# One line of due steps for ScalarE, VectorE and GpSimd, with their shared port in the planner, and epsilon added on ScalarE

## The chip, the cores and the metric

One core of one Trainium2 chip runs the whole program. The metric is device time in microseconds (us), the median of several executions of one compiled kernel. The engines are named as the profile names them: PE is TensorE, DVE is VectorE, ACT is ScalarE, POOL is GpSimd, SP issues the transfers.

## The reference

Local attention with a few global columns, followed by two feed-forward layers, all in float32:

```
attention: B=2, H=8, S=768, D=64; a query sees itself and the 95 keys before it, and the first 8 keys
  scores = q k^T / 8 - slope_h * distance, masked; a = exp(scores - max); a = a / (sum(a) + 1e-9); x = a v
layer 1:   1536 tokens, 512 -> 1536 -> 512:   x = ((x w_a) * (x w_b)) w_out
layer 2:   1536 tokens, 512 -> 2048 -> 512:   h = x w_in
           g = h where h >= 1, 0 where h <= -1, else (h + 1)^2 / 4;   out = g w_out
```

The weights arrive as float64. The matmuls of the two layers keep float32 accuracy by splitting each operand into a high and a low part and adding three products.

## The kernel before

**Work.** The 1536 tokens are three tiles of 512 (`t` = 0, 1, 2). Attention is cut into 24 units, each two heads by 256 queries; eight units make the input of one tile. A unit goes through PE and the other engines in turn: scores on PE (L681); mask, scale and row minimum on DVE out of PSUM (`least`, L698); four `exp` on ACT (L710); epsilon added to the four row sums (`add`, L718) and their reciprocal (`inverse`, L721) on DVE; four multiplications of rows by it (`norm`, L737) on POOL or DVE; transposes on PE (L745) and their copy out of PSUM on ACT or DVE; values on PE (L762); high part (ACT or DVE) and low part (DVE, L644) of the layer's input. Three units may be in flight.

A block of weights (`prep`, 68 of them, 128x512 each) is turned from float64 into a high and a low float32 by a chain of seven steps: L378 on ACT, L379 to L382 on DVE (L379 may be on POOL), a rounding copy `w_hlh` (L391 on DVE, L389 on ACT) and a subtraction `w_hll` (L384, on POOL or DVE). Only twelve such blocks have a place until the first product of the third tile. Products of a layer are 12 matmuls of 512 columns; the results are taken out of PSUM by `after_ab` and `evacuate` (L505, L519, L522, L527, L563) and split into `midh` and `midl` (L391/L389 and L410).

**Order.** Everything is emitted as one static program. A planner, `Clock`, decides the order while the program is built. It keeps a model time in ns; PE's part of the program advances it by `MM` for each matmul. Every step of the other three engines is handed to `Clock.on` with a slack (which gives its due time), its cost on each engine that could do it, and a function that tells when it may go. In the kernel before, `on` fixes the engine at once: it takes the one with the least sum of busy time, queued earlier-due work, cost and a handicap (`BIAS`, or `BIAS_W` for steps of slack 1900 and more; on DVE 900 and 1000 ns). `begin` then serves three separate queues by due time whenever the model says that an engine is free. Steps of DVE and POOL never exclude each other in this model. Each engine runs its instructions strictly in the order emitted, and waits by semaphores. PE's order is decided in `tile_kernel`: a step of the attention goes before the next matmul of a layer when it is due or when that matmul's operands are not there yet in the model.

The numbers that the change touches:

```
MM = 216
BIAS = dict(scalar=100, vector=900, gpsimd=0)
BIAS_W = dict(scalar=2700, vector=1000, gpsimd=200)
SLACK = dict(
    qk=400, reduce=0, exp=0, share=-800, norm=1000, turn=0, x=0, evac=1000, mid=3500, y=100, weights=500, soon=1900,
)
```

Of the kernel before, what the change touches and what calls it, by code (L numbers as in the profile page):

```python
# [2 lines left out]

# [11 lines left out]
AF = mybir.ActivationFunctionType  # L15
# [31 lines left out]
TINY, HUGE = 3.0517578125e-05, 122880.0  # L47


MM = 216  # L50
COPY = dict(scalar=520, vector=335)
COPY_PS = dict(scalar=478, vector=602)
SUB = dict(vector=602, gpsimd=1225)
CLAMP = dict(vector=335, gpsimd=1883)

BIAS = dict(scalar=100, vector=900, gpsimd=0)
BIAS_W = dict(scalar=2700, vector=1000, gpsimd=200)

HOP = dict(tensor=200, scalar=160, vector=170, gpsimd=120)
DMA = dict(issue=475, begin=1125, rate=360, end=900)  # L60
# [47 lines left out]
class Clock:  # L108

    ENGINES = ("scalar", "vector", "gpsimd")

    def __init__(self, nc):
        self.nc = nc
        self.now, self.seq, self.events = 0, 0, []
        self.busy = dict.fromkeys(self.ENGINES, 0)
        self.queue = {e: [] for e in self.ENGINES}
        self.dma_issue = self.dma_busy = -1 << 20  # L120
        self.poll = lambda: None

# [1 line left out]
        self.seq += 1  # L124
        heapq.heappush(self.events, (self.now + ns, self.seq, fn))

    def on(self, slack, emit, then=None, need=None, **costs):


        def end(e):  # L130
            ahead = sum(op[2] for op in self.queue[e] if op[0] <= self.now + slack)
            return max(self.busy[e], self.now) + ahead + costs[e] + (BIAS if slack < SLACK["soon"] else BIAS_W)[e]

        e = min(costs, key=end)
        self.seq += 1
        self.queue[e].append((self.now + slack, self.seq, costs[e], emit, then, need))

    def begin(self):

        more = True  # L140
        while more:
            more = False
            for e in self.ENGINES:
                if self.busy[e] > self.now:
                    continue
                for op in sorted(self.queue[e], key=lambda op: op[:2]):
                    _, _, ns, emit, then, need = op
                    if need and not need():
                        continue
                    self.queue[e].remove(op)  # L150
                    emit(getattr(self.nc, e))
                    self.busy[e] = self.now + ns
                    self.after(ns, lambda: None)
                    if then:
                        self.after(ns + HOP[e], then)
                    more = True
                    break

    def dma(self, n, then):
        issued = max(self.dma_issue, self.now)  # L160
# [127 lines left out]
class Ffn:  # L288
# [194 lines left out]
    def after_ab(self, kind, t, f, n, ps, room):  # L483
        clock = self.clock
        give = lambda: self.give(room)
        if kind == "a":
            a = []

            def emit(e):
                self.take("s1")  # L490
                a.append(self.p_s.tile([P, T], F32, tag="s1", name=f"a{n}"))
                self.copy(e, a[0], ps)

            def there():
                give()
                self.a[t, f] = a[0]

            clock.on(SLACK["evac"], emit, there, self.has("s1"), **COPY_PS)
        elif kind == "b":
            ab = []  # L500

            def emit(e):
                self.take("s2")
                ab.append(self.p_s.tile([P, T], F32, tag="s2", name=f"ab{n}"))
                e.tensor_tensor(ab[0], ps, self.a.pop((t, f)), ALU.mult)  # L505

            def there():
                give()
                self.give("s1")
                self.split_mid(("y", t, f), ab[0])  # L510

            clock.on(SLACK["evac"], emit, there, lambda: self.room["s2"] > 0 and (t, f) in self.a, vector=602)
        else:
            c, g = [], []

            def clip(e):
                self.take("s1")
                c.append(self.p_s.tile([P, T], F32, tag="s1", name=f"c{n}"))
                e.tensor_scalar(c[0], ps, -1.0, 1.0, ALU.max, ALU.min)  # L519

            def square(e):
                e.activation(c[0], c[0], AF.Square, bias=self.half, scale=0.5)  # L522

            def larger(e):
                self.take("s2")
                g.append(self.p_s.tile([P, T], F32, tag="s2", name=f"g{n}"))
                e.tensor_tensor(g[0], ps, c[0], ALU.max)  # L527

            def there():
                give()  # L530
                self.give("s1")
                self.split_mid(("o", t, f), g[0])

            s = SLACK["evac"]
            third = lambda: clock.on(s, larger, there, self.has("s2"), vector=602)
            second = lambda: clock.on(s, square, third, scalar=613)
            clock.on(s, clip, second, self.has("s1"), vector=598)

    def evacuate(self, kind, t, first, last, e, ps, cols):
        nc, clock = self.nc, self.clock  # L540
        if first:

            def copy(en):
                self.part[kind, t, e] = part = self.p_part.tile([P, T], F32, tag="part", name=f"{kind}part{t}_{e}")
                self.copy(en, part, ps)

            clock.on(SLACK["evac"], copy, lambda: self.give("acc"), **COPY_PS)
            return
        part = self.part[kind, t, e]

        def there():
            self.give("acc")
            if not last:
                return
            if kind == "o":
                row = t * T + e * P
                nc.sync.dma_start(self.out[row : row + P, cols], part[:, cols])
                return
            if t not in self.y:
                self.y[t] = self.new_x(f"y{t}")  # L560
            self.split(SLACK["y"], lambda: self.y[t][e], part, lambda at: self.ready.add(("h", t, e)))

        add = lambda en: en.tensor_tensor(part[:, cols], ps[:, cols], part[:, cols], ALU.add)  # L563
        clock.on(SLACK["evac"], add, there, vector=602)

    def prepare(self):

# [43 lines left out]
class Attention:  # L611
# [20 lines left out]
    def to_x(self, ps, t, p, col, w):  # L632

        ready, clock = self.ffn.ready, self.clock

        def then():
            self.give(ps)
            self.done[t, p] = self.done.get((t, p), 0) + w
            if self.done[t, p] == T:
                ready.update((kind, t, p) for kind in "ab")  # L640

        places = [a[:, col : col + w] for a in self.ffn.x[t][p]]
        hi = lambda e: self.ffn.copy(e, places[0], ps[:, :w])
        lo = lambda e: e.tensor_tensor(places[1], ps[:, :w], as_f32(places[0]), ALU.subtract)  # L644
        low = lambda: clock.on(SLACK["x"], lo, then, vector=335)
        clock.on(SLACK["x"], hi, low, scalar=264, vector=335)


class Window(Attention):
# [38 lines left out]
    def reduce(self, st, j, r, ps):  # L688
        clock = self.clock
        at, w = self.places(st)[r]  # L690
        i = st["i0"] + r
        m0 = (0, P, P + self.W)[min(i, 2)]
        pt, stat = st["p", j][:, at : at + w], st["stat"]
        n = NQ * j + r
        most, total = stat[:, 0, n : n + 1], stat[:, 1, n : n + 1]

        def least(e):
            e.tensor_tensor_reduce(  # L698
                pt, ps[:, at : at + w], self.masks.m[:, m0 : m0 + w], scale=-(0.5 ** (2 * st["p"] + j + 1)),
                scalar=3e38, op0=ALU.add, op1=ALU.min, accum_out=most,  # L700
            )

        def reduced():
            st["read", j] = st.get(("read", j), 0) + 1
            if st["read", j] == NQ:
                self.give(ps)
            clock.on(SLACK["exp"], exp, share, scalar=2 * w)

        def exp(e):
            e.activation(pt, pt, AF.Exp, bias=most, scale=-1.0, accum_out=total)  # L710

        def share():
            st["exp"] = st.get("exp", 0) + 1
            if st["exp"] == 2 * NQ:
                clock.on(SLACK["share"], add, lambda: clock.on(SLACK["share"], inverse, norms, vector=81), vector=70)

        def add(e):
            e.tensor_scalar_add(stat[:, 2], stat[:, 1], EPS)  # L718

        def inverse(e):  # L720
            e.reciprocal(stat[:, 2], stat[:, 2])  # L721

        def norms():
            for jj in range(2):
                for rr in range(NQ):
                    clock.on(SLACK["norm"], *self.norm(st, jj, rr), gpsimd=457, vector=202)

        clock.on(SLACK["reduce"], least, reduced, lambda: not i or not self.masks.left, vector=w * 4 // 3)

    def norm(self, st, j, r):  # L730
        at, w = self.places(st)[r]
# [7 lines left out]
    def turn(self, st, j):  # L739
# [9 lines left out]
            st["turned", j] = True  # L749

        copy = lambda e: self.ffn.copy(e, pt[:, :n], ps[:, :n])
        self.write(n * 110 // P, lambda: clock.on(SLACK["turn"], copy, out, scalar=52 + n * 5 // 6, vector=n * 7 // 6))

    def values(self, st):

# [366 lines left out]
```

## Time and profile before

| | |
|---|---|
| median of 3 runs | 666.62 us (664.29 to 666.94) |
| profiled execution | 665.21 us, of it 663.3 us from the first to the last instruction |
| busy: PE / DVE / ACT / POOL | 642.2 / 463.5 / 199.4 / 236.5 us |
| share of PE in the chain that ended last | 81%; DVE 15% |
| granted PE clock, mean | 0.991 |

Busy times are those of the profiled execution. PE's busy time holds the latency of each matmul and is no measure of how full PE is; the steps of the chain that ended last are. A DVE or POOL instruction that stands still while it holds its engine counts as busy.

### The profile page before, as it was taken

How to read it: one execution, taken by the hardware profiler on the slowest of the kernel's cores; microseconds unless marked ns; L12 is line 12 of the kernel's file. 1: busy time of each engine (PE TensorE's matmuls, PEld its weight loads, DVE VectorE, ACT ScalarE, POOL GpSimd, SP SyncE). 2: the span in 40 equal slices, each digit the busy share in tenths (PEclk: the TensorE clock that was granted, in tenths of full speed). 3: DMA queues.
4: the chain of work that ended last, by engine and by line, in shares of the span. 5: the costliest groups of instructions: out<-in, count | busy, mean ns of one | idle time of the engine just before them, and what ended most of it. 6: DMA issues, size and time to landing. Idle time of an engine off the chain costs nothing.

```text
span 663.3 us, 9060 instructions
## 1 busy us (share of the span) xinstructions
PE 642.2 (97%) x3190; PEld 514.1 (78%) x3190; DVE 463.5 (70%) x966; ACT 199.4 (30%) x458; POOL 236.5 (36%) x239
## 2 busy tenths in 40 slices
PE   6988899999999999999999999999999999999997
PEld 3665677778878888888888878888888888888886
DVE  7999966427792755982737997894699778944442
ACT  5766755542221201211212134333221212111110
POOL 4655744023252331331333445444241423222220
PEclk7899999999999999999999999999999999999999
DMA  7765652101341221430211330322121211000112
GB/s 218 221 199 171 178 174 74 48 1 64 96 126 33 63 64 33 127 96 0 68 59 41 120 95 1 127 65 64 33 96 63 65 40 56 0 1 17 48 49 84
DMA packets 23766, 52.71 MB, mean 79 GB/s; under 512 B 3104, under 2 KB 11552, under 8 KB 23712
## 3 DMA queue, kind: packets, MB, share of 16 engines
q1 hardware_dynamic: 23568, 52.05, 25.6%
q8 instruction: 27, 0.44, 0.3%
q14 instruction: 27, 0.22, 0.1%
q10 hardware_dynamic: 144, 0.00, 0.0%
HBM read 48.89 MB, written 3.15 MB: 78 GB/s over the span
## 4 chain that ended last, share of the span: by engine, by line
PE 81%; DVE 15%; issue 1%; ACT 0%; POOL 0%; DVEq 0%; POOLq 0%
PE ps L446 42%; PE o L474 20%; PE y L474 13%; PE at L762 2%; DVE p L698 2%; DVE bits L381 2%; PE at L681 2%; PE at L745 2%; DVE bits L382 1%; DVE bits L380 1%; DVE w_hlh L391 1%; DVE p L737 1%; DVE bits L379 1%; DVE midh L391 1%; DVE ab L505 1%
## 5 line engine op out<-in xcount | busy, mean ns | idle before, releaser
L384 POOL TENSOR_TENSOR w_hll<-bits,w_hlh 128x512 fp32r<-128x512 f32 x46 | 65.8, 1431 | 92.0 <-DVE w_hlh L391 83.5
L446 PE MATMUL ps<-xhx,w_hlh 128*128 128x512 f32 x224 | 88.5, 395 | 0.0
L446 PE MATMUL ps<-xlx,w_hlh 128*128 128x512 f32 x224 | 88.4, 394 | 0.0
L446 PE MATMUL ps<-xhx,w_hll 128*128 128x512 f32 x224 | 88.0, 393 | 0.0
L522 ACT ACTIVATE c<-c,half 128x512 f32<-128x512 f32 x48 | 34.8, 724 | 153.5 <-DVE c L519 153.5
L505 DVE TENSOR_TENSOR ab<-ps,a 128x512 f32<-128x512 f32 x34 | 23.4, 688 | 65.1 <-PE ps L446 65.1
L446 PE MATMUL ps<-xhy,w_hll 128*128 128x512 f32 x168 | 65.4, 389 | 0.0
L446 PE MATMUL ps<-xly,w_hlh 128*128 128x512 f32 x168 | 65.4, 389 | 0.0
L446 PE MATMUL ps<-xhy,w_hlh 128*128 128x512 f32 x168 | 65.4, 389 | 0.0
L378 ACT ACTIVATE bits<-raw 128x512 f32<-128x512 f32 x68 | 44.9, 669 | 64.0 <-POOL w_hll L384 43.3
L410 POOL TENSOR_TENSOR midl<-g,midh 128x512 fp32r<-128x512 f32 x25 | 33.6, 1344 | 84.2 <-DVE midh L391 84.2
L519 DVE TENSOR_SCALAR c<-ps 128x512 f32<-128x512 f32 x48 | 32.9, 686 | 42.1 <-PE ps L446 42.1
L382 DVE SCALAR_TENSOR_TENSOR bits<-raw,bits 128x512 uint32<-128x512 uint32 x68 | 52.6, 777 | 0.9
L527 DVE TENSOR_TENSOR g<-ps,c 128x512 f32<-128x512 f32 x48 | 33.1, 689 | 27.1 <-ACT c L522 25.6
L410 POOL TENSOR_TENSOR mid_morel<-g,mid_moreh 128x512 fp32r<-128x512 f32 x21 | 28.8, 1369 | 62.4 <-DVE mid_moreh L391 57.4
L381 DVE SCALAR_TENSOR_TENSOR bits<-raw,bits 128x512 uint32<-128x512 uint32 x68 | 49.6, 735 | 0.6
L446 PEld LDWEIGHTS ps<-xhx,w_hlh 128*128 128x128 f32 x224 | 42.1, 188 | 9.7 <-issue 1.7
L446 PEld LDWEIGHTS ps<-xlx,w_hlh 128*128 128x128 f32 x224 | 42.1, 188 | 8.9 <-issue 1.0
L446 PEld LDWEIGHTS ps<-xhx,w_hll 128*128 128x128 f32 x224 | 42.1, 188 | 8.6 <-issue 0.3
L389 ACT COPY a<-ps 128x512 f32<-128x512 f32 x34 | 19.9, 585 | 88.3 <-PE ps L446 84.5
L410 POOL TENSOR_TENSOR midl<-ab,midh 128x512 fp32r<-128x512 f32 x15 | 19.6, 1306 | 59.6 <-DVE midh L391 58.8
L380 DVE TENSOR_SCALAR bits<-bits 128x512 uint32<-128x512 uint32 x68 | 40.0, 593 | 0.9
(296 smaller groups left out, 1477.6 us busy)
## 6 DMA issues: line engine op xcount, KB each, us to landing
raw<-in_wu SPq DMA_DIRECT2D x68, 512.0 KB, 3.6
v<-in_vd SPq DMA_DIRECT2D x16, 256.0 KB, 3.8
k<-in_k SPq DMA_DIRECT2D x16, 200.0 KB, 3.8
q<-in_qd SPq DMA_DIRECT2D x48, 64.0 KB, 3.7
out<-opart SPq DMA_DIRECT2D x11, 256.0 KB, 2.0
k<-in_k SPq DMA_DIRECT2D x8, 128.0 KB, 3.5
v<-in_vd SPq DMA_DIRECT2D x8, 128.0 KB, 3.5
v<-in_vd SPq DMA_DIRECT2D x8, 64.0 KB, 3.4
```

What stands on the lines that cost most here:

```text
L378: (lambda e: e.activation(as_f32(b), as_f32(high), AF.Abs), dict(scalar=520)),
L380: (lambda e: e.tensor_scalar(b, b, 3, 0x3FFFFFF8, shl, both), dict(vector=335)),
L381: (lambda e: e.scalar_tensor_tensor(b, low, 29, b, shr, or_), dict(vector=602)),
L382: (lambda e: e.scalar_tensor_tensor(b, high, 0xC0000000, b, both, or_), dict(vector=602)),
L384: (lambda e: e.tensor_tensor(wl, as_f32(b), as_f32(wh), ALU.subtract), SUB),
L410: e.tensor_tensor(at[1], src, as_f32(at[0]), ALU.subtract)
L446: nc.tensor.matmul(ps, l, r, start=c == 0 and m == 0, stop=last)
L474: nc.tensor.matmul(ps[:, cols], l, r[:, cols], start=f == lo and m == 0, stop=last)
L505: e.tensor_tensor(ab[0], ps, self.a.pop((t, f)), ALU.mult)
L519: e.tensor_scalar(c[0], ps, -1.0, 1.0, ALU.max, ALU.min)
L522: e.activation(c[0], c[0], AF.Square, bias=self.half, scale=0.5)
L527: e.tensor_tensor(g[0], ps, c[0], ALU.max)
```

## The change

Four things, in the planner and in one step of the attention.

1. `Clock.on` puts every step in one line, sorted by due time, with its costs on all engines and a flag `port`. The engine is chosen when a step can start. `one` goes through the line: for each step that may go, it finds the engine that would end it first, given what earlier-due steps have reserved. If that engine can start it now, it is emitted; if not, the engine's time (and the port's) is reserved up to its end, and the next step is looked at.
2. In this model a POOL step, and a DVE step unless marked otherwise, needs the port that the two share: only one of them runs at a time. Marked as not needing it are steps that read PSUM (`least`, L505, L519, L527, L563, L644, copies out of PSUM) and the reciprocal.
3. Handicaps are all zero, and some costs are new: `MM` 227, `exp` 100 + 25/16 of its columns, L644 and its copy 315, the reciprocal 85.
4. Epsilon is added by an activation on ACT instead of a DVE instruction.

```diff
-MM = 216
+MM = 227
-BIAS = dict(scalar=100, vector=900, gpsimd=0)
-BIAS_W = dict(scalar=2700, vector=1000, gpsimd=200)
+BIAS = dict(scalar=0, vector=0, gpsimd=0)
...
-        self.queue = {e: [] for e in self.ENGINES}
+        self.port = 0
+        self.line = []
...
+    def on(self, slack, emit, then=None, need=None, port=True, **costs):
         self.seq += 1
-        self.queue[e].append((self.now + slack, self.seq, costs[e], emit, then, need))
+        bisect.insort(self.line, (self.now + slack, self.seq, costs, port, emit, then, need))
...
+    def one(self):
+        now = self.now
+        free = {e: max(t, now) for e, t in self.busy.items()}
+        if all(t > now for t in free.values()):
+            return False
+        gate = max(self.port, now)
+        for n, op in enumerate(self.line):
+            _, _, costs, port, emit, then, need = op
+            if need and not need():
+                continue
+            best = None
+            for e, ns in costs.items():
+                shared = e == "gpsimd" or e == "vector" and port
+                at = max(free[e], gate) if shared else free[e]
+                if best is None or at + ns + BIAS[e] < best[0]:
+                    best = at + ns + BIAS[e], at, e, ns, shared
+            _, at, e, ns, shared = best
+            if at <= now:
+                del self.line[n]
+                emit(getattr(self.nc, e))
+                self.busy[e] = now + ns
+                if shared:
+                    self.port = now + ns
+                self.after(ns, lambda: None)
+                if then:
+                    self.after(ns + HOP[e], then)
+                return True
+            free[e] = at + ns
+            if shared:
+                gate = at + ns
+        return False
...
-        low = lambda: clock.on(SLACK["x"], lo, then, vector=335)
-        clock.on(SLACK["x"], hi, low, scalar=264, vector=335)
+        low = lambda: clock.on(SLACK["x"], lo, then, None, False, vector=315)
+        clock.on(SLACK["x"], hi, low, None, False, scalar=264, vector=315)
...
-            clock.on(SLACK["exp"], exp, share, scalar=2 * w)
+            clock.on(SLACK["exp"], exp, share, scalar=100 + w * 25 // 16)
...
-                clock.on(SLACK["share"], add, lambda: clock.on(SLACK["share"], inverse, norms, vector=81), vector=70)
+                clock.on(SLACK["share"], add, lambda: clock.on(SLACK["share"], inverse, norms, None, False, vector=85), scalar=200)
...
-            e.tensor_scalar_add(stat[:, 2], stat[:, 1], EPS)
+            e.activation(stat[:, 2], stat[:, 1], AF.Copy, bias=EPS)
```

What is not shown of the diff hands `False` for the port to the steps named under 2. No transfer, tile, buffer, matmul or slack is changed.

## Rows read from the trace of the kernel before

**Rows 1.** Busy time by stage: PE, PEld, DVE, ACT, POOL; PE clock, DMA share, GB/s

```profile
25.00:95.00 70.00, 62.95 (x484) 43.82 (x484) 68.82 (x229) 48.83 (x159) 45.89 (x63) 1.00 0.64 190
95.00:146.00 51.00, 51.00 (x350) 37.65 (x350) 22.40 (x86) 27.36 (x78) 12.00 (x20) 1.00 0.16 46
146.00:391.65 245.65, 243.60 (x1077) 200.76 (x1074) 167.69 (x258) 47.58 (x81) 79.02 (x58) 1.00 0.23 71
391.65:644.64 252.99, 252.99 (x1118) 209.46 (x1117) 180.44 (x298) 59.30 (x91) 87.39 (x63) 1.00 0.15 49
```

**Rows 2.** PE's attention matmuls from 25 to 95 us, by line: busy, mean ns | idle

```profile
L745 PE MATMUL at<-ident,p 128*128 128x128 f32 x100 | 17.2, 284 | 5.3 <-POOL p L737 3.2 <-DVE st__852 L698 1.0 <-DVE p L737 0.7
L681 PE MATMUL at<-k,q 64*128 64x256 f32 (+1 forms) x104 | 14.8, 383 | 0.8 <-DVE st__556 L698 0.8
L762 PE MATMUL at<-p,v 128*64 128x128 f32 x196 | 13.8, 279 | 0.7 <-DVE xlx L644 0.4 <-ACT p L389 0.4
```

**Rows 3.** Chain that ended last, 100 to 131 us: start, length, what

```profile
101.07 1.02 PE at L762 x16
...
103.44 1.06 PE at L681 x8
...
111.62 0.44 PE at L745 x4
112.05 0.93 PE y L474 x4
```

**Rows 4.** PE's attention matmuls from 95 to 146 us, by line

```profile
L762 PE MATMUL at<-p,v 128*64 128x128 f32 x124 | 8.5, 279 | 0.0
L745 PE MATMUL at<-ident,p 128*128 128x128 f32 x56 | 8.4, 272 | 0.0
L681 PE MATMUL at<-k,q 64*128 64x256 f32 x48 | 6.8, 402 | 0.0
```

**Rows 5.** What PE's weight loads waited for, 25 to 95 us: total, times, longest

```profile
PEld at L745 <- POOL p L737: 7.5, 16, 1.2
```

**Rows 6.** DVE from 25 to 95 us, by line

```profile
L381 DVE SCALAR_TENSOR_TENSOR bits<-raw,bits 128x512 uint32<-128x512 uint32 x10 | 7.9, 785 | 0.1
L382 DVE SCALAR_TENSOR_TENSOR bits<-raw,bits 128x512 uint32<-128x512 uint32 x10 | 7.8, 782 | 0.0
...
L391 DVE CAST w_hlh<-bits 128x512 fp32r<-128x512 f32 x10 | 4.2, 418 | 0.0
```

**Rows 7.** Line L718, epsilon: duration min/median/max in ns, start

```profile
L718 DVE TENSOR_SCALAR st__556<-st__556 x1: 163/163/163, 37.8 to 37.8; 128x4 f32<-128x4 f32 x1
L718 DVE TENSOR_SCALAR st__588<-st__588 x1: 1242/1242/1242, 41.9 to 41.9; 128x4 f32<-128x4 f32 x1
```

**Rows 8.** Instructions in order of time around 41 us: start, length, engine

```profile
41.30 0.68 DVE L381 SCALAR_TENSOR_TENSOR bits<-raw,bits 128x512 uint32<-128x512 uint32 x1
...
41.47 1.65 POOL L384 TENSOR_TENSOR w_hll<-bits,w_hlh 128x512 fp32r<-128x512 f32 x1 [2.18 <-DVE w_hlh L391]
...
41.90 1.24 DVE L718 TENSOR_SCALAR st__588<-st__588 128x4 f32<-128x4 f32 x1
```

**Rows 9.** Line L698: duration min/median/max in ns

```profile
L698 DVE CUSTOM_DVE_ANT_0 p<-at,masks x96: 277/415/425, 7.9 to 132.2; 128x256 f32<-128x256 f32 x80, 128x128 f32<-128x128 f32 x16
```

**Rows 10.** L718 alone, 25 to 95 us: DVE busy and count

```profile
25.00:95.00 70.00, 8.11 (x14) 1.00 0.64 190
```

**Rows 11.** L710, exp of one unit on ACT: duration min/median/max in ns

```profile
L710 ACT ACTIVATE p<-p,st__270 x4: 387/447/493, 8.3 to 9.5; 128x128 f32<-128x128 f32 x2, 128x256 f32<-128x256 f32 x2
L710 ACT ACTIVATION_READ_ACCUMULATOR p<-p,st__270 x4: 185/187/188, 8.6 to 9.9; 128x1 f32 x4
```

**Rows 12.** L737, norms, alone, 25 to 95 us: DVE busy, POOL busy

```profile
25.00:95.00 70.00, 8.34 (x20) 25.59 (x40) 1.00 0.64 190
```

**Rows 13.** L737 by unit: duration min/median/max in ns

```profile
L737 POOL TENSOR_SCALAR p<-p,st__925 x4: 478/479/644, 71.8 to 73.8; 128x256 f32<-128x256 f32 x4
...
L737 DVE TENSOR_SCALAR p<-p,st__556 x3: 278/343/344, 39.3 to 39.8; 128x256 f32<-128x256 f32 x2, 128x128 f32<-128x128 f32 x1
```

**Rows 14.** L384, weight subtraction, whole run: duration min/median/max in ns

```profile
L384 POOL TENSOR_TENSOR w_hll<-bits,w_hlh x46: 1272/1337/2273, 20.2 to 558.6; 128x512 fp32r<-128x512 f32 x46
...
L384 DVE TENSOR_TENSOR w_hll<-bits,w_hlh x14: 677/1030/1667, 18.3 to 574.9; 128x512 fp32r<-128x512 f32 x14
```

**Rows 15.** POOL from 25 to 95 us, by line

```profile
L384 POOL TENSOR_TENSOR w_hll<-bits,w_hlh 128x512 fp32r<-128x512 f32 x8 | 11.6, 1455 | 5.8 <-DVE w_hlh L391 5.4 <-DVE st__762 L721 0.4
```

More of the change, by code (lines that the diff above doesn't have):

```diff
@@ L1 @@
+import bisect
+import heapq
 from contextlib import ExitStack
-import heapq
 import concourse.bass as bass
@@ L125, in after @@
         heapq.heappush(self.events, (self.now + ns, self.seq, fn))
[L127 to L134, printed above, removed]
+    def on(self, slack, emit, then=None, need=None, port=True, **costs):
         self.seq += 1
-        self.queue[e].append((self.now + slack, self.seq, costs[e], emit, then, need))
+        bisect.insort(self.line, (self.now + slack, self.seq, costs, port, emit, then, need))
@@ L138, in begin @@
     def begin(self):
[L140 to L157, printed above, removed]
+        while self.one():
+            pass
@@ L496, in there @@
                 self.a[t, f] = a[0]
-            clock.on(SLACK["evac"], emit, there, self.has("s1"), **COPY_PS)
+            clock.on(SLACK["evac"], emit, there, self.has("s1"), False, **COPY_PS)
         elif kind == "b":
@@ L510, in there @@
                 self.split_mid(("y", t, f), ab[0])
-            clock.on(SLACK["evac"], emit, there, lambda: self.room["s2"] > 0 and (t, f) in self.a, vector=602)
+            clock.on(SLACK["evac"], emit, there, lambda: self.room["s2"] > 0 and (t, f) in self.a, False, vector=602)
         else:
@@ L534, in after_ab @@
             s = SLACK["evac"]
-            third = lambda: clock.on(s, larger, there, self.has("s2"), vector=602)
+            third = lambda: clock.on(s, larger, there, self.has("s2"), False, vector=602)
             second = lambda: clock.on(s, square, third, scalar=613)
-            clock.on(s, clip, second, self.has("s1"), vector=598)
+            clock.on(s, clip, second, self.has("s1"), False, vector=598)
     def evacuate(self, kind, t, first, last, e, ps, cols):
@@ L545, in copy @@
                 self.copy(en, part, ps)
-            clock.on(SLACK["evac"], copy, lambda: self.give("acc"), **COPY_PS)
+            clock.on(SLACK["evac"], copy, lambda: self.give("acc"), None, False, **COPY_PS)
             return
@@ L563, in evacuate @@
         add = lambda en: en.tensor_tensor(part[:, cols], ps[:, cols], part[:, cols], ALU.add)
-        clock.on(SLACK["evac"], add, there, vector=602)
+        clock.on(SLACK["evac"], add, there, None, False, vector=602)
     def prepare(self):
@@ L726, in norms @@
                     clock.on(SLACK["norm"], *self.norm(st, jj, rr), gpsimd=457, vector=202)
-        clock.on(SLACK["reduce"], least, reduced, lambda: not i or not self.masks.left, vector=w * 4 // 3)
+        clock.on(SLACK["reduce"], least, reduced, lambda: not i or not self.masks.left, False, vector=w * 4 // 3)
     def norm(self, st, j, r):
@@ L751, in turn @@
         copy = lambda e: self.ffn.copy(e, pt[:, :n], ps[:, :n])
-        self.write(n * 110 // P, lambda: clock.on(SLACK["turn"], copy, out, scalar=52 + n * 5 // 6, vector=n * 7 // 6))
+        self.write(n * 110 // P, lambda: clock.on(SLACK["turn"], copy, out, None, False, scalar=52 + n * 5 // 6, vector=n * 7 // 6))
     def values(self, st):
```

## The prediction

> **What bounds the kernel now.** I read the stages first [rows 1]. From 95 us on PE is the bound: its instructions follow each other without a gap, and from 391.65 to 644.64 us 1118 of them take 252.99 us, 0.226 us each. At that pitch the 1077 of the stage from 146 us would need 243.7 of 245.65 us, so at least 1.9 us is lost there. Nothing that other engines do can make these stages shorter than that. From 25 to 95 us it is otherwise: DVE is busy for 68.8 of 70 us.
>
> How much PE loses there I work out from what its work takes where it never waits. In the chain that ended last, eight score matmuls take 1.06 us, sixteen value matmuls 1.02, four transposes 0.44, four matmuls of a layer 0.93 [rows 3]. From 25 to 95 us PE ran 104, 196 and 100 of the first three [rows 2], and 484 in all [rows 1], so 84 of a layer: 13.8 + 12.5 + 11.0 + 19.5 = 56.8 us. The same sum over 95 to 146 us, with 48, 124 and 56 [rows 4] and so 122 of a layer, gives 6.4 + 7.9 + 6.2 + 28.4 = 48.9 of 51 us in which PE waited for nothing; the rest is the change from one kind to another. Scaled by 51/48.9 the first stage holds 59.2 us of work. PE loses 11 to 13 us there, and that is nearly all there is to gain. Its largest listed wait is for POOL's norms, 7.5 us in 16 times [rows 5].
>
> DVE's 68.8 us are not all work. An addition on 128x4 takes 163 ns in one unit and 1242 ns in the next [rows 7]. In order of time [rows 8]: POOL's subtraction is listed from 41.47 us, while DVE's L381 runs to 41.98; POOL ends at 43.12; DVE's addition, from 41.90 us, ends at 43.14. POOL needs 1272 ns alone [rows 14], so it stood until DVE was done, and then DVE stood until POOL was done. Steps of both that touch only SBUF exclude each other. L698, which reads PSUM, never takes over 425 ns in 96 times [rows 9]: such steps are not held. The change's model says just this, and the model before does not.
>
> **Part by part.**
> *Epsilon to ACT.* In the stage 14 additions cost DVE 8.1 us [rows 10]; they leave it entirely. On ACT the nearest rows bound one from 185 ns (a read of 128x1) to 387 ns (an exp of 128x128) [rows 11]; I take 0.2 us, as 128x4 is nearest to 128x1. That is 2.8 us (bounds 2.6 to 5.4) on an engine busy for 48.8 of 70. Behind the addition on ACT stand the next unit's exps and the copies of transposes, each 0.2 us later; the reciprocal on DVE now waits for ACT, and L698 stands behind it. The planner issues it only after a hop of 160 ns, so I charge nothing for that; if ACT runs late by more, DVE stands for the difference.
>
> The Trainium skill, "ScalarE: Activation LUTs", section "Rules for kernel authors", speaks against this step: additions belong on VectorE. By that page's figure for an activation with immediate operands (section "What ACT_TABLE_LOAD costs") one would take an estimated 0.19 us, so 24 of them against 163 ns would lose 0.6 us of engine time. The trace agrees with the rule only for the additions that meet no POOL step.
>
> *The port in the model.* L381 and L382 take 0.78 us in the stage [rows 6]; alone L381 took 0.68 [rows 8], so 20 of them stand for 2 us; 20 norms at 417 ns [rows 12] against 343 [rows 13] for 1.5. Of these 3.5 us I count 2 as gained, since the port still has to be waited for, only planned. Bounds: 0 and 3.5.
>
> *No handicaps, engine chosen late.* Two shifts. Ten rounding copies of 0.42 us on DVE [rows 6] may go to ACT: I take a third, 1.4 us off DVE (bounds 0 and 4.2). Against this, POOL did 40 norms and 8 weight subtractions [rows 12, 15], and a DVE that is free ends them sooner: 343 against 478 ns, 677 against 1272 [rows 13, 14]. If all came to DVE it would carry 40 x 0.343 + 8 x 0.677 = 19.1 us more, if none, 0. But where earlier-due steps have reserved DVE, POOL ends first and is taken; four L698 reserve 1.4 us in the model. I take a third, 6.4 us. The port gains by this too, since POOL's 45.9 us of holding or waiting for it [rows 1] shrink. Norms done sooner also shorten the wait of rows 5.
>
> *Costs and MM.* They change the order alone. 227 ns is the pitch that rows 1 show, so the model's PE no longer runs ahead of the chip's by 5% where PE is the bound. I count nothing: PE's own queue covers it there, and if that cover went, the 1.9 us lost from 146 us would grow.
>
> *Sum.* DVE needs 68.8 - 8.1 - 2 - 1.4 + 6.4 = 63.7 us in the stage in place of 68.8. At the same fullness (98%) the stage takes 64.8, a gain of 5.2 us; PE's 57 to 59 us still fit. The bounds of the shares move this from nothing (all of POOL's steps, no copy moved) to 11 us, where PE is full. Of the 1.9 us from 146 us on I count 1.5 as gained, by the same relief: DVE and POOL prepare weights in bursts there. Before 25 us one unit's norms come sooner, 0.8 us (bounds 0 and 2). Together 7.5 us: 663.3 - 7.5 = 655.8 us of span, and with the 1.9 us around it 657.7 against the profiled 665.2. The median of the runs lies 1.4 above the profiled time, which would make it 659.1; between the two I take 658.
>
> **Rivals.**
> *ACT becomes the bound.* With 2.8 us of additions and all ten copies at 0.5 us, ACT carries 56.6 us in a stage of 65: 87%, with four exps in a row for each unit. Exps and transposes' copies then come late, and PE waits for them. For it: ACT is already busy for 70% of the stage [rows 1]. Against: the planner knows its costs, and takes ACT only where it ends first. Price: 3 to 5 us of the gain, 661 to 663.
>
> *The reservations leave DVE idle (the other side).* When a due step wants the port and POOL holds it, the model reserves DVE up to that step's end, and later-due steps that read PSUM and could run at once are not let in front. Before, DVE stood in the same way by accident; now it would by plan. Without the addition and its waits DVE has 57 us of steps in the stage (68.8 - 8.1 - 3.5), so it breaks even at 13 us of such idling, 28% of POOL's 45.9 us. At 45% it is 21 us, a stage of 78, and a time of 673. For it: POOL's single subtraction holds for 1.27 us, as long as three L698. Against: more steps that take the port go to DVE itself, which never gates itself.
>
> *The loss re-forms.* Three units in flight, each a chain through PE, DVE, ACT and POOL: when DVE is relieved, the length of that chain can be what PE waits for, and the twelve places for weights fill no faster. Then the 8 us come off DVE and not off PE: 664 to 667. For it: DVE has idle time after 95 us, which PE there does not need. Against: DVE is at 98%, not at 85.
>
> *PE full from 25 us on.* All 11 to 13 us and the later 1.9 are won: 650 to 653. For it: DVE would need to fall only to 58 us.
>
> **How the numbers follow.** Chances: forecast (654 to 661) 0.54, ACT as the bound 0.16, idle reservations 0.13, the loss re-forms 0.09, PE full 0.08. A measurement here tells about 0.5%, 3.3 us, from no change: faster means under 663.3, slower over 670. ACT as the bound falls into faster by two thirds. Faster: 0.54 + 0.08 + 0.11 = 0.73; same: 0.05 + 0.09 = 0.14; slower: 0.13. The range 650 to 667 leaves out the idle reservations, and a little at the lower end and of the re-formed loss, together under 0.2. The forecast's own range is 654 to 661.
>
> **What would show it.** L718 is an ACT line of some 0.2 us, 24 times, and no DVE instruction on 128x4 takes over 0.3 us. Durations of L381, L382 and L380 lie near their least in most instances. Norms are mostly on DVE, and PE's waits for POOL's norms fall from 7.5 us to under 3. ACT does some of the rounding copies. The work that PE did by 95 us is done by about 89. From 391 us on, nothing differs. I am wrong if DVE shows idle time while PE waits before 90 us, or if PE shows new waits after 146 us.

## The result, and the profile after

The changed kernel takes 659.83 us (659.75 to 661.12, 5 runs) against 666.62: a ratio of 0.991, interval 0.9888 to 0.9933. That is 6.8 us between medians; the profiled executions differ by 4.9 (660.28 against 665.21) and their spans by 4.8 (658.5 against 663.3). The forecast was 658, with 650 to 667 around it.

The two differences are not the same. The kernel before spreads, and the mean clock that PE was granted over the span spreads with it: of its 42 executions beside the experiments below, the 23 at 0.988 or less took 666.6 to 668.8 us, the 19 at 0.990 or more 664.1 to 666.7. The profiled one, at 0.991, belongs to the faster; the changed kernel's five lie at 0.988 to 0.993. So some 2 of the 6.8 us are not in the two profiles compared here, and no trace shows where in the span they lie.

Busy time by stage, as in [rows 1]; the last two stages are cut at the same products as there (they end 4.7 us sooner):

```profile
25.00:95.00 70.00, 66.77 (x509) 45.75 (x509) 70.00 (x256) 52.48 (x177) 20.60 (x33) 1.00 0.62 183
95.00:146.00 51.00, 51.00 (x343) 37.78 (x340) 31.27 (x107) 26.69 (x80) 2.00 (x4) 1.00 0.22 67
146.00:386.95 240.95, 240.95 (x1064) 199.49 (x1064) 163.83 (x300) 62.56 (x104) 0.00 (x0) 1.00 0.23 73
386.95:639.90 252.95, 252.95 (x1117) 209.45 (x1117) 186.57 (x320) 78.19 (x122) 0.00 (x0) 1.00 0.15 49
```

From 25 to 95 us PE runs 25 instructions more than before (509 against 484). But DVE did not become less full: it is busy for all 70 us. What changed is POOL: 20.6 us here in place of 45.9, and nothing at all after 146 us.

Before 25 us the changed kernel falls behind. The score matmuls up to there, in the kernel before and then in the changed one (busy, mean ns | idle):

```profile
L681 PE MATMUL at<-k,q 64*128 64x256 f32 (+1 forms) x40 | 6.4, 450 | 2.8 <-DMA k<-in_k 1.9 <-POOL q L243 0.8
```

```profile
L694 PE MATMUL at<-k,q 64*128 64x256 f32 (+1 forms) x34 | 6.8, 486 | 5.9 <-DMA k<-in_k 5.7 <-issue 0.2
```

It has run six score matmuls and one matmul of a layer fewer by 25 us. By the prediction's price of each kind of matmul that is an estimated 1.0 us of work less. From 25 to 95 us its 110 score matmuls, 212 of values, 100 transposes and 87 of a layer are worth an estimated 59.3 us against 56.8 before, 2.5 more.

Two places in the chain that ended last give the stages to a hundredth. After the attention's last values, PE runs 60 matmuls of a layer in one unbroken piece, in both kernels of the same products; the last piece is 72 matmuls. The kernel before, then the changed one (start, length, what):

```profile
146.42 13.85 PE ps L446 x60
...
644.64 13.76 PE o L474 x72
```

```profile
144.62 13.85 PE ps L459 x60
...
639.90 13.76 PE o L487 x72
```

So 1.8 us came before the unbroken piece, and between the two pieces 498.22 us became 495.28: 2.94 more. Together 4.7. In the kernel before PE waits twice between them (total, times, longest), in the changed kernel never; these two lines name 2.0 of the 2.94 us:

```profile
PE y L474 <- DVE midl L410: 1.2, 1, 1.2
PE ps L446 <- DVE ab L505: 0.8, 1, 0.8
```

The additions of epsilon on ACT, as in [rows 7], the first of 24:

```profile
L731 ACT ACTIVATE st__270<-st__270 x1: 195/195/195, 11.1 to 11.1; 128x4 f32<-128x4 f32 x1
```

The norms from 25 to 95 us, as in [rows 12] (DVE busy, POOL busy), and DVE's lines in that stage: those that answer to [rows 6], the copies of transposes, the copies `xhx`, of which DVE had none before, and the norms of one unit:

```profile
25.00:95.00 70.00, 15.57 (x44) 7.86 (x16) 1.00 0.62 183
```

```profile
L394 DVE SCALAR_TENSOR_TENSOR bits<-raw,bits 128x512 uint32<-128x512 uint32 x9 | 6.3, 695 | 0.0
...
L395 DVE SCALAR_TENSOR_TENSOR bits<-raw,bits 128x512 uint32<-128x512 uint32 x8 | 5.8, 728 | 0.0
L404 DVE COPY p<-at 128x384 f32<-128x384 f32 (+1 forms) x10 | 5.6, 569 | 0.0
...
L404 DVE CAST xhx<-at 128x256 fp32r<-128x256 f32 x8 | 3.3, 409 | 0.0
L750 DVE TENSOR_SCALAR p<-p,st__654 128x256 f32<-128x256 f32 x3 | 2.2, 795 | 0.0
...
L404 DVE CAST w_hlh<-bits 128x512 fp32r<-128x512 f32 x2 | 0.8, 411 | 0.0
```

The copies of transposes that DVE did before the change:

```profile
L391 DVE COPY p<-at 128x384 f32<-128x384 f32 (+1 forms) x5 | 2.9, 598 | 0.0
```

The two-operand steps hardly stand still any more (0.70 and 0.73 us against 0.785 and 0.782). Most norms came to DVE: 44 of 60 in place of 20. Most rounding copies left it, 2 in place of 10; but eight copies `xhx` and five more copies of transposes came to it from ACT. DVE is as full as it was, with work in place of most of the waits; some are left, such as those of the three norms above, 795 ns on average (343 in [rows 13]). What PE's weight loads waited for POOL's norms fell from 7.5 us [rows 5] to 0.5.

### The profile page after: what moved, and what is told of

It is laid out like the page before. It is cut to its first block, busy times and chain, and to the rows that moved or that the text cites. A ratio compares the mean times of both kernels' runs of the same rounds, so it can differ in the third digit from the quotient of the medians.

```text
span 658.5 us, 8812 instructions
## 1 busy us (share of the span) xinstructions
PE 643.0 (98%) x3190; PEld 514.4 (78%) x3190; DVE 476.5 (72%) x1071; ACT 234.8 (36%) x528; POOL 28.3 (4%) x64
## 4 chain that ended last, share of the span: by engine, by line
PE 90%; DVE 5%; DMA 3%; SPq 1%; issue 1%; ACT 0%; DVEq 0%
PE ps L459 48%; PE o L487 20%; PE y L487 15%; PE at L775 2%; PE at L694 2%; PE at L758 2%; DVE p L711 1%; DMA v<-in_vd 1%; DMA k<-in_k 1%; DVE p L750 1%; PE e L609 1%; SPq L275 1%; DMA raw<-in_wu 1%; DVE bits L395 1%; DVE xlx L657 0%
## 5 line engine op out<-in xcount | busy, mean ns | idle before, releaser
L402 ACT COPY a<-ps 128x512 f32<-128x512 f32 x28 | 16.4, 587 | 95.5 <-PE ps L459 91.7
L395 DVE SCALAR_TENSOR_TENSOR bits<-raw,bits 128x512 uint32<-128x512 uint32 x68 | 46.4, 689 | 0.5
L394 DVE SCALAR_TENSOR_TENSOR bits<-raw,bits 128x512 uint32<-128x512 uint32 x68 | 46.1, 686 | 0.3
L402 ACT CAST w_hlh<-bits 128x512 fp32r<-128x512 f32 x46 | 28.4, 620 | 48.0 <-DVE bits L395 47.9
L397 DVE TENSOR_TENSOR w_hll<-bits,w_hlh 128x512 fp32r<-128x512 f32 x54 | 36.9, 685 | 1.7
L487 PE MATMUL y<-midh,w_hll 128*128 128x512 f32 x96 | 37.9, 394 | 0.0
L487 PE MATMUL y<-midh,w_hlh 128*128 128x512 f32 x96 | 37.8, 394 | 0.0
L487 PE MATMUL y<-midl,w_hlh 128*128 128x512 f32 x96 | 37.7, 392 | 0.0
```

Of the source, the lines that this page charges most:

```text
L394: (lambda e: e.scalar_tensor_tensor(b, low, 29, b, shr, or_), dict(vector=602)),
L395: (lambda e: e.scalar_tensor_tensor(b, high, 0xC0000000, b, both, or_), dict(vector=602)),
L397: (lambda e: e.tensor_tensor(wl, as_f32(b), as_f32(wh), ALU.subtract), SUB),
L402: e.copy(dst, src)
L487: nc.tensor.matmul(ps[:, cols], l, r[:, cols], start=f == lo and m == 0, stop=last)
```

## The experiments

Each edit is against the kernel named; each run has its ratio to the kernel before on the same chip, with a 95% interval. The columns behind it are read from each profile like the two pieces above: the start of the unbroken run, and the time from there to the last piece. "POOL +400" is an advantage of 400 ns in the planner's choice. With 800 ns for POOL a break divides the run of 60; 141.56 is the start of the piece behind it, less the 13.85 us of an unbroken run.

| run | us | ratio, interval | first run at | from there to the last piece | POOL busy | DVE busy, 25 to 95 us |
|---|---|---|---|---|---|---|
| before | 666.5 to 666.8 | 1 | 146.42 | 498.22 | 236.5 | 68.82 |
| changed | 659.83 | 0.991 (0.9888 to 0.9933) | 144.62 | 495.28 | 28.3 | 70.00 |
| before, epsilon on ACT | 662.0 | 0.9926 (0.9912 to 0.9939) | 142.87 | 498.27 | 241.4 | 63.67 |
| before, MM 227 | 666.5 | 1.0001 (0.9987 to 1.0015) | 148.16 | 498.21 | 232.1 | 68.25 |
| before, no handicaps | 660.22 | 0.9902 (0.9882 to 0.9921) | 145.31 | 495.31 | 66.3 | 69.84 |
| before, no handicaps, POOL +400 | 663.26 | 0.9945 (0.9927 to 0.9963) | 143.53 | 498.39 | 168.8 | 69.97 |
| changed, epsilon back | 659.25 | 0.9883 (0.9868 to 0.9898) | 143.10 | 495.29 | 25.9 | 69.92 |
| changed, no port | 660.53 | 0.9906 (0.9891 to 0.9921) | 143.69 | 495.45 | 86.4 | 69.46 |
| changed, 400 against DVE | 655.12 | 0.9826 (0.9812 to 0.9839) | 138.62 | 495.28 | 118.5 | 55.71 |
| changed, ACT +400 | 656.67 | 0.985 (0.9828 to 0.9873) | 140.14 | 495.30 | 27.7 | 69.65 |
| changed, POOL +400 | 654.07 | 0.9806 (0.9787 to 0.9826) | 138.04 | 495.29 | 114.3 | 60.33 |
| changed, POOL +400, epsilon back | 658.31 | 0.9873 (0.9852 to 0.9894) | 142.13 | 495.30 | 118.0 | 60.08 |
| changed, POOL +800 | 657.89 | 0.9872 (0.9851 to 0.9892) | 141.56 | 495.29 | 285.4 | 52.80 |
| changed, POOL +400, no port | 664.61 | 0.9966 (0.9953 to 0.9979) | 143.24 | 500.75 | 166.3 | 67.40 |

**Epsilon alone, on the kernel before.**

```diff
-            e.tensor_scalar_add(stat[:, 2], stat[:, 1], EPS)
+            e.activation(stat[:, 2], stat[:, 1], AF.Copy, bias=EPS)
...
-                clock.on(SLACK["share"], add, lambda: clock.on(SLACK["share"], inverse, norms, vector=81), vector=70)
+                clock.on(SLACK["share"], add, lambda: clock.on(SLACK["share"], inverse, norms, vector=81), scalar=200)
```

> The kernel before with one edit: epsilon is added on ScalarE (200 ns in the planner). The working of the prediction says that VectorE bounds 25 to 95 us and that the 14 additions there cost it 8.1 us; then this alone gives 5 us or more, 661 us or less, and the stage before the first unbroken run of matmuls (146.4 us in the kernel before) ends 5 us sooner. Rival, from the profile after, where that stage ended only 1.8 us sooner: what VectorE saves is used up by another wait, GpSimd's norms above all, and the time is 665 to 667.

662.0 us, 4.8 less. The stage, 25 to 95 us:

```profile
25.00:95.00 70.00, 65.45 (x518) 46.26 (x515) 63.67 (x219) 52.74 (x180) 48.74 (x66) 1.00 0.65 189
```

DVE falls by 5 us while PE does 34 instructions more in the same time, and the unbroken run starts 3.55 us sooner. The later stage does not move. The mechanism is as forecast, the size a little under the 5 us expected; a part of what DVE saves becomes idle time, and 3.55 of the 8.1 us reach PE.

**Epsilon back, in the changed kernel.**

```diff
-            e.activation(stat[:, 2], stat[:, 1], AF.Copy, bias=EPS)
+            e.tensor_scalar_add(stat[:, 2], stat[:, 1], EPS)
...
-                clock.on(SLACK["share"], add, lambda: clock.on(SLACK["share"], inverse, norms, None, False, vector=85), scalar=200)
+                clock.on(SLACK["share"], add, lambda: clock.on(SLACK["share"], inverse, norms, None, False, vector=85), vector=70)
```

> The changed kernel with epsilon back on VectorE, now planned as a step that needs the port. If the addition itself was dear, the time goes back by 3 us or more, to 663 or over. If it was dear only because GpSimd held the port, then with GpSimd nearly idle (28 us busy in the whole run) it costs 24 x 0.1 us of VectorE in a stage that VectorE bounds, some 2 us: 661 to 662.

659.25 us: both sides of the expectation had some loss, and there is none; its interval overlaps that of the changed kernel. What is worth 4.8 us alone is worth nothing inside the change. With POOL nearly idle an addition on DVE takes 154 to 170 ns in the 20 that the profile lists.

**The port left out of the model.**

```diff
-                shared = e == "gpsimd" or e == "vector" and port
+                shared = False
```

> The changed kernel with the port left out of the planner's model: any step of GpSimd and VectorE may run at once in it. If the port is what the change gains by, GpSimd gets many steps again, the waits on VectorE come back (L394 and L395 well over 0.69 us on average) and the time is that of before, 664 to 668. If the one line and the late choice of the engine do it, the time stays within 2 us of 659.8.

660.53 us, not to be told from the changed kernel. The port in the model did nothing here.

**MM alone, on the kernel before** (`MM = 227`).

> The kernel before with MM 227 alone. The prediction counted nothing for it: 666 to 668. Rival: the waits of TensorE that the kernel before has between 146 and 391 us (2.9 us, gone in the changed kernel) come from a planner that thinks TensorE 5% too fast; then they go here too, the stage from the first unbroken run of 60 matmuls to the last of 72 falls from 498.2 to 495.3 us, and the time to 664.

666.5 us, ratio 1.0001: nothing, as the prediction had it. The rival's 495.3 us did not come either: the later stage takes 498.21.

**No handicaps, on the kernel before.**

```diff
-BIAS = dict(scalar=100, vector=900, gpsimd=0)
-BIAS_W = dict(scalar=2700, vector=1000, gpsimd=200)
+BIAS = dict(scalar=0, vector=0, gpsimd=0)
+BIAS_W = dict(scalar=0, vector=0, gpsimd=0)
```

> The kernel before with all handicaps zero and its engines still fixed at once. If the missing handicap is what brings all steps to VectorE and rounding copies to ScalarE, GpSimd falls under 100 us busy here too, and the stage after 146 us takes 495.3 us: 661 to 664. If it needs the late choice as well, GpSimd keeps over 150 us and the time is 665 to 669; it may be worse, since a step is then fixed to a VectorE that the model thinks free while GpSimd holds the port.

660.22 us. Six zeros give the whole gain of the change, with the old queues, no port in the model and epsilon on DVE. (No run keeps the old handicaps in the changed planner, and none sets the zeros one engine at a time.) POOL falls to 66 us, and the later stage takes 495.31 us:

```profile
145.31 13.87 PE ps L446 x60
...
640.62 13.76 PE o L474 x72
```

**Shares moved back: to ACT and POOL, to POOL alone, to ACT alone**, in the changed kernel, by one of the three added lines each.

```diff
-BIAS = dict(scalar=0, vector=0, gpsimd=0)
+BIAS = dict(scalar=0, vector=400, gpsimd=0)
+BIAS = dict(scalar=0, vector=0, gpsimd=-400)
+BIAS = dict(scalar=-400, vector=0, gpsimd=0)
```

> The changed kernel with a handicap of 400 ns on VectorE, so that GpSimd gets steps again while the model still keeps the two apart on the port. In the changed kernel VectorE is busy for all of 25 to 95 us and GpSimd for 20 of these 70. If VectorE's fullness is what is left of the loss, VectorE falls under 95% there and 2 to 5 us are won: 655 to 658. If the port is the real bound, each step on GpSimd holds it twice as long and nothing is won or some is lost: 660 to 664.

> The changed kernel with an advantage of 400 ns for GpSimd alone; steps that ScalarE and VectorE can do are chosen as in the changed kernel. If GpSimd's share is what VectorE lacked, this gives most of the 4.7 us that the handicap of 400 ns gave: 655 to 657. If ScalarE's copies gave them, 659 to 662, with VectorE still at 95% or more from 25 to 95 us.

> The changed kernel with an advantage of 400 ns for ScalarE alone. If copies on ScalarE are what helps, 655 to 657, with VectorE under 90% from 25 to 95 us; if GpSimd's steps are, 659 to 661. ScalarE as the next bound would show as 662 or more, with TensorE waiting for copies of transposes.

655.12, 654.07 and 656.67 us. All three gain, and all of it before the unbroken run, which starts 4.5 to 6.6 us sooner than in the changed kernel. So work taken off DVE, by either neighbour, wins time that the change leaves lost. That the fullness of DVE as such is this loss is not shown: with ACT favoured DVE stays at 69.65 us and the unbroken run starts at 140.14, while two runs below have DVE at 60.08 and 52.80 us and start it at 142.13 and 141.56. POOL alone gives the least time of this study, 0.9806 of the kernel before; its interval overlaps that of the 400 ns against DVE. Its stages, with the same columns as above:

```profile
25.00:95.00 70.00, 69.38 (x535) 49.91 (x531) 60.33 (x212) 56.87 (x186) 46.44 (x85) 1.00 0.62 180
138.04:633.33 495.29, 495.29 (x2186) 410.11 (x2186) 337.39 (x588) 140.50 (x227) 43.67 (x32) 1.00 0.19 60
```

POOL is as busy in the first stage as it was before the change (45.9 us), and PE does 535 instructions there, not 484. The run that favours ACT fits neither expectation whole: its time is that of "copies are what helps", but DVE stays at 69.65 us. It is as full as before and does more of what only DVE can do: 20 of the steps L394 and L395 in the stage, not 17. Part of this gain comes early: PE runs 516 instructions in the stage, not 509, but 626 by 95 us, not 601. ACT is nowhere as full as DVE was: its most is 57.74 of 70 us, in the run with 400 ns against DVE.

**The same, with each other part taken out.** POOL's 400 ns without the port; with epsilon back on DVE; in the kernel before, with its three queues; and 800 ns.

> The changed kernel with an advantage of 400 ns for GpSimd and the port left out of the model. The changed kernel without the port lost only 0.7 us, but there GpSimd was busy for 86 us. If the port in the model is worth something once GpSimd is used, GpSimd takes over 180 us here, VectorE's steps stand behind it again and 5 us or more are lost against the same advantage with the port: 659 to 665. If the model's port is worth nothing anywhere, 653 to 656.

> The advantage of 400 ns for GpSimd and epsilon back on VectorE, planned as a step that needs the port. If epsilon on ScalarE is worth its 4.8 us only where GpSimd blocks it unplanned, this stays within 1.5 us of 654.1. If it is worth something wherever GpSimd is used, 657 to 659.

> The kernel before, its three queues and engines fixed at once, with no handicap but an advantage of 400 ns for GpSimd. If the handicaps are all that matters, 654 to 657. If one line with the port is what lets GpSimd be used without blocking VectorE, GpSimd is used here too, VectorE's steps show waits (L381 and L382 well over 0.69 us on average), and the time is 660 to 666.

> The changed kernel with 800 ns for GpSimd. If VectorE's fullness is still what is lost, 651 to 653. If the port and GpSimd's own slowness take over (a subtraction holds the port 1.3 us there against 0.7), time is given back: 655 to 660, with VectorE less full than with 400 ns and TensorE waiting for GpSimd.

*Without the port:* 664.61 us, 10.5 more than with it; 5.2 of that lie before the unbroken run, 5.5 behind it. POOL takes 166 us, not over 180 as expected, and DVE's two-operand steps wait again (over the whole run, then the same with the port):

```profile
L395 DVE SCALAR_TENSOR_TENSOR bits<-raw,bits 128x512 uint32<-128x512 uint32 x68 | 55.2, 820 | 0.7
L394 DVE SCALAR_TENSOR_TENSOR bits<-raw,bits 128x512 uint32<-128x512 uint32 x68 | 48.5, 721 | 0.7
```

```profile
L395 DVE SCALAR_TENSOR_TENSOR bits<-raw,bits 128x512 uint32<-128x512 uint32 x68 | 46.8, 692 | 0.6
L394 DVE SCALAR_TENSOR_TENSOR bits<-raw,bits 128x512 uint32<-128x512 uint32 x68 | 46.7, 693 | 0.7 <-DMA q<-in_qd 0.3
```

PE then waits after 143 us (total, times, longest); with the port in the model it waits nowhere there:

```profile
PE ps L459 <- DVE g L540: 1.2, 1, 1.2
PE ps L459 <- DVE ab L518: 1.1, 1, 1.1
PE o L487 <- POOL mid_morel L423: 0.7, 1, 0.7
PE ps L459 <- DVE a L404: 0.6, 1, 0.6
```

*Old queues:* 663.26 us, with the later stage at 498.39 and L382 at 913 ns on average. *Epsilon back:* 658.31 us, 4.2 more: epsilon on ACT is worth something again as soon as POOL works. But the additions hardly stand still there (the longest of the 20 listed takes 455 ns), and DVE is no fuller (60.08 against 60.33 us). So these 4.2 us are not the blocking that the same edit removed from the kernel before. DVE waits for the exps in front of nine of the additions, 5.2 us in all, in the whole run; but with epsilon on ACT it waits as long, 6.0 us in front of six reciprocals, for the additions there. So this wait is not the difference either, and the cause of the 4.2 us stays open. *800 ns:* 657.89 us. DVE falls to 52.8 of 70 us and PE does 520 instructions, not 535:

```profile
25.00:95.00 70.00, 66.90 (x520) 47.43 (x519) 52.80 (x191) 55.69 (x184) 52.50 (x85) 1.00 0.59 174
```

More of POOL than balances DVE gives time back, as expected. Yet POOL's 285 us in the whole run leave the later stage at 495.29: with the port in the model POOL's use costs PE nothing there. It is not that DVE's steps no longer stand behind POOL's. Over the whole run they take longer than without the port above:

```profile
L395 DVE SCALAR_TENSOR_TENSOR bits<-raw,bits 128x512 uint32<-128x512 uint32 x68 | 56.8, 847 | 0.7
L394 DVE SCALAR_TENSOR_TENSOR bits<-raw,bits 128x512 uint32<-128x512 uint32 x68 | 56.3, 839 | 0.4
```

They wait, and PE's operands are there in time all the same. A plan that counts the waiting would do that; no run shows it apart from the other changes of order. In the kernel before and the four others without the port in the model in which POOL is busy for 166 to 241 us, the stage takes 498.2 to 500.8.

## Why the prediction was right or wrong

The time and its direction were right: 659.83 against 658, inside 654 to 661. That it came so close is in part luck. The gain before the unbroken piece was 1.8 us in place of 6.0 (5.2 and 0.8), the gain behind it 2.94 in place of 1.5, and some 2 of the 6.8 us between the medians are in neither. In the profiles alone 4.8 us of span were won, and 7.5 were forecast.

*What bounds the kernel.* Right. From 386.95 us on 1117 matmuls take 252.95 us, as in [rows 1]. All that moved lies before 95 us and in the 2 to 3 us lost from 146 to 391.

*Epsilon.* The addition takes 189 to 209 ns in the 20 that the profile of the changed kernel lists; 0.2 was taken. The estimate of 0.19 us from the figure of the Trainium skill ("ScalarE: Activation LUTs", section "What ACT_TABLE_LOAD costs") agrees with that. The Trainium skill's rule on the same page, to add on VectorE (section "Rules for kernel authors"), does not hold for the kernel before, where the edit alone wins 4.8 us; inside the change, where POOL is nearly idle, it costs nothing to follow it.

*The step that failed:* the load of DVE under "No handicaps, engine chosen late", and with it DVE's 63.7 us. Epsilon left DVE as counted, 8.1 us. POOL's share was put at 6.4 us, "a third"; 24 of the 40 norms came, 7.2 us (8.34 to 15.57), and one weight subtraction more, 0.5. The rounding copies were put at 1.4 us off DVE and took off 3.4 (4.2 to 0.8). The largest error is a term put at nothing: copies that came to DVE from ACT, 3.3 us of `xhx` and 2.7 more of transposes, 6.0 together. Five more of the weight step L379 add 1.6 (2.06 to 3.63). L381 and L382 take 4.2 less (15.7 to 11.5), in part because three fewer ran. So some 15 us left DVE (8.1, 3.4 and 4.2) and about as much came (7.2, 0.5, 6.0 and 1.6): DVE did not fall to 63.7 us but stayed at 70.0 of 70, and the stage gave an estimated 2.5 us in place of 5.2.

Why ACT's copies came can be read from the planner's costs: `xhx` is put at 264 ns on ACT and 315 on DVE (335 before), and before the change 100 and 900 were added to these, so that now DVE is taken as soon as ACT is busy for 51 ns longer. With 400 ns in favour of ACT two copies `xhx` and six of transposes are left on DVE, not eight and ten.

The argument for a third was that four reserved L698 make POOL end first. It holds only while such steps are ready together; in the other instants DVE ends a norm first, and by more in the planner's costs (202 against 457) than in the durations that the prediction compared (343 against 478 ns). The rule takes the engine that ends one step first, not the one that is less needed.

*Before 25 us* 0.8 us was counted as gained; an estimated 1.0 us of PE's work was lost there. What it was lost to is not shown: PE waits for the transfer of `k` for 5.7 us in place of 1.9, but no longer for the 3.1 us in front of transposes that the kernel before has there. By 95 us PE is then an estimated 1.5 us of work ahead, not the 6 that the prediction named as a sign.

*A bound of the sum* does not follow from its own terms: with all of POOL's steps and no copy moved it gives 68.8 - 8.1 - 2 + 19.1 = 77.8 us on DVE, a loss of 8 to 9 us, not "nothing".

*The later stage* was put at 1.5 us and gave 2.94. That is all there was: no kernel here takes less than 495.28 us from one piece to the other. In the change it is not the model of the port that did it, since 495.45 us come out without it, but that POOL has no work there: 0.00 us. Without handicaps in the old queues it comes out the same.

*The port.* Costed at 2 us, as waits that would go. Most of them went, but by disuse of POOL; with the port out of the model the time is the same. Only where POOL is kept in use was the model worth anything, and there it is 10.5 us.

*MM.* Nothing, as counted.

*The rivals.* ACT did not become the bound (52.5 of 70 us). The reservations did not leave DVE idle: it was busy without a break, so the price of that rival was never tested in the change. "The loss re-forms" was in part what happened: the 8 us came off DVE and were filled again, though by POOL's steps and ACT's copies and not by the length of the units' chains.

## What to carry to other kernels

A change that lets a planner see a conflict can gain by never meeting it: look first at who does the work now, then at whether the new model is used at all. Choosing for each step the engine that ends it first loaded the fastest engine here until it was full; a handicap on an engine is a price for its time, and has to be set again when the model changes (here an advantage of 400 ns for POOL is worth 5.8 us with the port in the model, and in the old planner, against no handicap, costs 3.0). Test each part alone and each part taken out, since one worth 4.8 us alone was worth nothing beside the others.

## What the runs showed of the hardware

POOL and DVE hold each other up on steps that touch only SBUF, planned apart or not. Over the whole run L395 takes 692 ns on average where POOL is busy for 114 us (with the port in the model), 820 where it is busy for 166 (without), and 847 where it is busy for 285 (with the port again). That a step as short as an addition on 128x4 is held as long as a whole subtraction on POOL (1242 ns for 163) was what made it dear in the kernel before; as an activation it varied by 20 ns (189 to 209).
